# Pooled attention with an affine MLP block: the order of the first batch, and one of four products per batch moved to GpSimd

## The chip, the cores and the metric

The kernel runs on one core of a Trainium2 chip. A core has TensorE (PE in the profile; its weight loads are PEld), VectorE (DVE), ScalarE (ACT), GpSimd (POOL) and SyncE (SP), each with its own queue of instructions in program order; they wait for each other through semaphores. The metric is device time in microseconds (us), the median of several runs.

## The reference

Eight batches of eight heads, 576 positions, 64 values per head. k and v are averaged over groups of 8 positions, which leaves 72 keys. The attention of all 576 queries over these keys is the input x of an MLP block that first mixes tokens and then channels.

```
k_p, v_p = mean over 8 positions of k, v          # 72 of each
attn = softmax(q @ k_p^T / 8);   x = attn @ v_p    # 576 x 512 per batch
u = x + lam * (w_tok @ (alpha1 * x + beta1))
out = u + lam * (relu((alpha2 * u + beta2) @ w_ch1) @ w_ch2)
```

## The kernel before

The order of all instructions is written out by hand. Tokens are cut into chunks of 128: a batch has four chunks of its own and half of a fifth, which it shares with its neighbour. Four chunks are a block of the channel MLP, and there are nine blocks. The first batch (batch 0) has its attention ahead of all blocks, in straight-line code (lines 654 to 739). Block n then carries the attention of batch n+1 in its gaps. There the functions below are put on a list `todo` with a due time, in units of one step of TensorE work (0 to 15 are the 16 units of the first layer, `mlp_A`; 16 to 31 the quarters of the second, `mlp_B`), and the list is sorted by it and emitted (lines 792 to 824). The due times for a batch are in `attention(b)` (lines 742 to 790).

The steps of the attention, by name:

- `att_F` and `att_Frem` bring q into transposed form (in the first two batches with TensorE transposes, later with DMA). `cast_rem` makes bf16 of the last 64 rows of q and k.
- `sum_k` (GpSimd) adds up k, `att_K` (TensorE, then a copy) does the pooling of four heads. `double_k` prepares k in batch 0. `first_V` and `att_V` pool v.
- `att_S` or `att_S4` computes scores; ACT takes the exponential into ET.
- `att_AV(b, h)` multiplies with v for one head: five matmuls into ps_av, then DVE takes a reciprocal (L525) and writes x_tm (L527).
- `att_X(b, h0, h1)` multiplies two heads of x_tm with lam * alpha1 (`lamal_bc`), giving xs: a wide product of four chunks (L534) and a small one of the 64 rows of the fifth chunk (L538). Four calls make a batch, one per pair of heads.
- `mix_T(b, c)` is the token mix of one chunk: matmuls of wtT and xs (L567), DVE adds x (L571), and a product with alpha2 (L574) gives u_bf; `mix_uT` transposes it for `mlp_A`. `mix_T(b, 0)` needs all of xs.
- `setup_wtok(c)` transposes w_tok for chunk c (TensorE, then an ACT copy, L299); `setup_rowsum(c)` adds its row sums (L308, ACT copy L310), `setup_wtok_odd` makes the copy for odd batches (L316, L319, L320). `setup_bias(g)` computes beta2 through the first layer.
- `broadcast` spreads a vector over 128 partitions: a matmul with a row of ones into ps_bc, then ACT or DVE takes it out. `keep_warm(n)` issues n matmuls whose result nobody reads.

Buffers: x_tm has one buffer, PSUM has a ring of six that most steps share in the order of their allocation (`gp`), and two for the second layer (`ps_ch`). Loads on GpSimd's queue convert to bf16 on the way. Some loads are held back by a small memset on DVE (`behind`), so that they start at a chosen place of DVE's order.

Of the kernel before, what the change touches and what calls it, by code (L numbers as in the profile page):

```python
# [7 lines left out]
FP = mybir.dt.float32  # L8
# [3 lines left out]
ALU = mybir.AluOpType  # L12
# [11 lines left out]
def kernel(  # L24
# [116 lines left out]
    def cast_rem(b, eng, copy=None):  # L141
        raw = st1[b]["rem_raw"]
        rq = work.tile([P, 2, 2, D], BF, tag="rem_q", bufs=2, name="rem_q")
        rk = work.tile([P, 2, 2 if b else 3, D], BF, tag="rem_k", bufs=2, name="rem_k")
        (copy or eng.tensor_copy)(out=rq.rearrange("p c h d -> p h c d"), in_=raw[:, 0])  # L145
        twice = [raw[:, 1, :, c].unsqueeze(2).to_broadcast((P, 2, 2, D)) for c in range(2)]
        if b:
            eng.tensor_tensor(out=rk, in0=twice[0], in1=twice[1], op=ALU.add)
        st1[b]["rem"] = rq, rk
# [27 lines left out]
    al2_bc = const.tile([P, DM], FP, tag="al2_bc", name="al2_bc")  # L177
    b2row = const.tile([4, P], FP, tag="b2row", name="b2row")

    vecs = const.tile([65, 4, DM], FP, tag="vecs", name="vecs")  # L180
    ones_row = const.tile([1, P], FP, tag="ones_row", name="ones_row")
    nc.vector.memset(ones_row, 1.0)

    def load_vector(i, src, queue=nc.scalar):
        n = 65 if i in (0, 3) else 1
        queue.dma_start(out=vecs[0:n:64, i],
                        in_=src.unsqueeze(0).to_broadcast((1 + n // 65, DM)))

    new_batch(0)
    load_vector(0, moe_lam)  # L190
    load_rem(0)
    load_q_bf(0, 0)
    load_k16(0, 0)
    load_vector(1, moe_alpha1, nc.sync)
    load_vector(3, moe_beta1, nc.sync)
    start = const.tile([1, 2], FP, tag="start", name="start")
    nc.vector.memset(start, 0.0)
    nc.scalar.activation(out=start[:, 1:2], in_=start[:, 0:1], func=AF.Exp, bias=0.0, scale=1.0)
# [56 lines left out]

    def bias_row(i):
        p0 = 64 - 64 * i
        nc.vector.tensor_tensor(out=xs_pool[i][p0:p0 + 1, 4, :], in0=vecs[p0:p0 + 1, 3],
                                in1=vecs[p0:p0 + 1, 0], op=ALU.mult)

    b2c_bf = const.tile([P, 4], BF, tag="b2c_bf", name="b2c_bf")
# [3 lines left out]
    def more_constants():  # L265
        nc.vector.memset(ones_bf, 1.0)
        nc.vector.memset(ones_lo[0:64], 1.0)
        nc.vector.memset(ones_lo[64:128], 0.0)
        nc.vector.memset(wtT[:, :, S:640], 0.0)
# [2 lines left out]
        behind.memset(al2_bc[:, 0:1], 0.0)  # L272
        nc.sync.dma_start(out=al2_bc, in_=moe_alpha2.unsqueeze(0).to_broadcast((P, DM)))

    def broadcast(i, out, by=None):

        ps = gp("ps_bc")
        nc.tensor.matmul(out=ps, lhsT=ones_row, rhs=vecs[0:1, i])
        if by is None:
            nc.scalar.copy(out=out, in_=ps)  # L280
        else:
            nc.vector.tensor_tensor(out=out, in0=by, in1=ps, op=ALU.mult)

    def setup_vectors():
        ps = gp("ps_vec")
# [68 lines left out]
    def att_F(b, hp, copy=nc.scalar.copy):  # L354


        st = st1[b]
        u, r = hp // 2, hp % 2
        if r == 0:
            st["qT"][u] = work.tile([P, 8, P], BF, tag="qT", bufs=4, name="qT")  # L360
        if b > 1:
            if r == 0:
                nc.sync.dma_start_transpose(out=st["qT"][u],
                                            in_=st["q"][u].rearrange("p h c d -> p (h c d)"))
            return
        ps_q = gp("ps_q").bitcast(BF)
        for c in range(4):
            nc.tensor.transpose(
                out=ps_q[:, 128 * c:128 * c + 128],
                in_=st["q"][u][:, 2 * r + c // 2, 2 * (c % 2):2 * (c % 2) + 2].rearrange(  # L370
                    "p c d -> p (c d)"),
                identity=identity_bf)
        copy(out=st["qT"][u][:, 4 * r:4 * r + 4, :],
                       in_=ps_q[:, 0:512].rearrange("p (c t) -> p c t", c=4))
# [152 lines left out]
        nc.vector.tensor_tensor(out=x[:, 1 - odd:6 - odd, dd:dd + D], in0=av[:, :, 0:64],  # L527
                                in1=rec.unsqueeze(2).to_broadcast((P, 5, D)), op=ALU.mult)

    def att_X(b, h0, h1, eng=nc.vector):  # L530

        x, xs = st1[b]["x"], xs_pool[b % 2]
        cols = slice(D * h0, D * h1)
        eng.tensor_tensor(  # L534
            out=xs[:, 0:4, cols], in0=x[:, 1:5, cols],
            in1=lamal_bc[:, cols].unsqueeze(1).to_broadcast((P, 4, D * (h1 - h0))), op=ALU.mult)
        p0 = 64 * (b % 2)
        eng.tensor_tensor(out=xs[p0:p0 + 64, 4, cols], in0=x[p0:p0 + 64, 5 - 5 * (b % 2), cols],  # L538
                          in1=lamal_bc[p0:p0 + 64, cols], op=ALU.mult)


    st2 = {}
# [11 lines left out]
    def keep_warm(count):  # L554

        ps = psB.tile([P, DM], FP, tag="ch", bufs=2, name="ps_warm")
        for _ in range(count):
            nc.tensor.matmul(out=ps, lhsT=warm[:, 0:P], rhs=warm)
# [98 lines left out]
    load_q_bf(1, 0)  # L657
    load_q_bf(1, 1)
    load_w1(2)
    keep_warm(2)  # L660
    broadcast(0, lam_bc)
    keep_warm(2)
    att_F(0, 0)
    att_F(0, 1)
    more_constants()
    cast_rem(0, nc.vector)
    att_Frem(0, nc.scalar.copy)
    keep_warm(1)
    double_k(0)
# [10 lines left out]
    keep_warm(1)  # L680
    att_K(0, 1, None)
    att_AV(0, 1)
    broadcast(1, lamal_bc, lam_bc)
    att_F(0, 2)
    att_F(0, 3, nc.vector.tensor_copy)
    att_X(0, 0, 2, nc.gpsimd)
    att_AV(0, 2)
    keep_warm(1)
    att_S(0, 4)
    first_V(0, 1)  # L690
    att_AV(0, 3)
    att_X(0, 2, 4, nc.gpsimd)
    load_al2(nc.vector)
    att_S(0, 5)
    setup_vectors()
    keep_warm(1)
    att_AV(0, 4)
    att_S(0, 6)
    keep_warm(1)
    att_AV(0, 5)  # L700
    load_rem(1, behind=nc.vector)
    att_X(0, 4, 6, nc.gpsimd)
    att_S(0, 7)
    setup_wtok(0, nc.scalar.copy)
    att_AV(0, 6)
    setup_wtok(1, nc.scalar.copy)
    att_AV(0, 7)
    for u in range(2):
        load_k(1, u, nc.vector)
    setup_rowsum(0)  # L710
    setup_wtok(2, nc.scalar.copy)
    setup_rowsum(1)
    setup_wtok(3, nc.scalar.copy)
    att_X(0, 6, 8)
    setup_rowsum(2)
    keep_warm(1)
    load_w1(3)
    load_v16(1, (0, 1))
    setup_rowsum(3)
    mix_T(0, 0, nc.gpsimd)  # L720
    mix_T(0, 1, nc.gpsimd)
    load_v16(1, (2,))
    for g in range(3):
        load_w2(g)
    setup_bias(0)
    mix_T(0, 2)
    mix_uT((0, 0))
    mix_T(0, 3)
    setup_wtok(4, nc.scalar.copy)
    mix_uT((0, 1))  # L730
    setup_bias(1)
    mlp_A(0, 0, 0, 256)
    mix_uT((0, 2))
    mlp_A(0, 1, 0, 256)
    mlp_A(0, 2, 0, 256)
    mix_uT((0, 3))
    mlp_A(0, 3, 0, 256)
# [4 lines left out]
    def attention(b):  # L742


        first = b == 1
        todo = []
        if first:
            for hp in range(4):
                todo.append((2.6 + 0.9 * hp, lambda hp=hp: att_F(b, hp)))
            todo.append((3.5, lambda: cast_rem(b, nc.gpsimd)))  # L750
            todo.append((3.65, lambda: load_w2(3)))
            todo.append((7.4, lambda: att_Frem(b, nc.scalar.copy)))
        if b < B - 1:
            at = 27.0 if first else 10.0
            todo.append((at, lambda: att_F(b + 1, 0)))
            todo.append((at + 0.1, lambda: att_F(b + 1, 2)))
            at = 28.0 if first else 25.5
            todo.append((at - 1.0, lambda: cast_rem(b + 1, nc.gpsimd)))
            todo.append((at, lambda: att_Frem(b + 1)))
        for u in range(2):  # L760
            todo.append((3.6 + 0.1 * u if first else -0.9 + 1.2 * u,
                         lambda u=u: sum_k(b, u, nc.gpsimd)))
            todo.append((6.4 + 3.0 * u if first else 4.1 + 2.0 * u,
                         lambda u=u: att_K(b, u, nc.vector.tensor_copy)))
            if first:
                todo.append((11.0 + 1.2 * u, lambda u=u: first_V(b, u)))
        for u in range(2):
            at = (9.0 if first else 6.3, 13.6)[u]
            todo.append((at, lambda u=u: att_S4(b, u)))
            for k, dt in enumerate((0.1, 0.1, 0.1, 0.7, 1.7, 1.75) if u else (0.1, 0.1, 0.1, 1.1, 2.1, 3.1)):  # L770
                todo.append((at + dt, lambda u=u, k=k: st1[b]["exp", u](k)))
            for i, dt in enumerate((2.9, 3.4, 4.6, 5.1) if u else (5.7, 6.2, 2.9, 3.4)):
                h = 4 * u + i
                todo.append((at + dt, lambda h=h: att_AV(b, h)))
                if i % 2:
                    todo.append((at + dt + 0.1, lambda h=h: att_X(b, h - 1, h + 1)))
        if not first:
            for hp in range(4):
                todo.append((0.2 + 2.0 * hp, lambda hp=hp: att_V(b, hp)))
        for c in range(5):  # L780
            at = 21.0 + 1.3 * c
            if c < 4 or b % 2:
                todo.append((at, lambda c=c: mix_T(b, c)))
                key = (b, c) if c < 4 else (b - 1, 4)
                if first and c in (2, 3):
                    at += 1.3 * c - 2.0
                elif first and c < 2:
                    at += 1.0
                todo.append((at + 1.8, lambda key=key: mix_uT(key)))
        return todo  # L790
# [64 lines left out]
```

The softmax here doesn't subtract the row's maximum and nothing guards it: scores larger than these inputs give would overflow.

## Time and profile before

The median is 354.74 us (352.35 to 355.02, three runs). In the profiled execution the span is 351.1 us.

| engine | busy us | instructions |
|---|---|---|
| PE | 337.8 | 2206 |
| DVE | 226.0 | 476 |
| ACT | 150.6 | 283 |
| POOL | 78.9 | 93 |

| product xs (att_X) | count | us of one |
|---|---|---|
| DVE, wide, 128x512 | 29 | 0.69 |
| DVE, small, 64x128 | 29 | 0.29 |
| POOL, wide | 3 | 1.27 |
| POOL, small | 3 | 0.44 to 0.90 |

The span begins with the attention of batch 0; the first token mix starts at 23.99 us and the first layer of block 0 at 30.5 us. In the stretch from 0 to 50 us the DMA engines are nearly always busy. The table by engine is an average over all this: it says little about a wait in one place, for which the chain (what released each step) and the timeline of one engine have to be read.

### The profile page before, as it was taken

The numbers are of one execution on the slowest core, as the hardware profiler recorded it, in microseconds if no ns is written. First come the engines' busy times: TensorE is split into PE (matmuls) and PEld (weight loads), VectorE is DVE, ScalarE is ACT, GpSimd is POOL, SyncE is SP. The second block draws the span as 40 slices with busy tenths as digits, with TensorE's granted clock in tenths as the row PEclk, the third lists the DMA queues.
The fourth block names the chain that finished last, engine by engine and source line by source line (L and its number), as shares of the span: only waits on it lengthen the run. The fifth ranks groups of instructions, "written<-read, shape, count | busy, mean of one in ns | idle before, by whom it ended". The sixth has DMA issues, their size and how long they took to land.

```text
span 351.1 us, 5881 instructions
## 1 busy us (share of the span) xinstructions
PE 337.8 (96%) x2206; PEld 178.8 (51%) x2247; DVE 226.0 (64%) x476; ACT 150.6 (43%) x283; POOL 78.9 (22%) x93
## 2 busy tenths in 40 slices
PE   7989999999999999999999999999999999999995
PEld 2667654455544554455445544554455445545544
DVE  6564048788696769775967697948785883037511
ACT  4564972238502850087008800791069105703800
POOL 8578600072017000710071005300510000000000
PEclk9999999999999999999999999999999999999999
DMA  8999980898738942897189719991820032011012
GB/s 129 196 213 241 217 151 0 188 248 174 134 113 203 216 63 66 231 190 121 55 224 189 127 52 211 186 146 51 228 75 1 32 90 77 0 60 62 0 54 66
DMA packets 66045, 44.57 MB, mean 127 GB/s; under 512 B 32409, under 2 KB 57309, under 8 KB 66018
## 3 DMA queue, kind: packets, MB, share of 16 engines
q1 hardware_dynamic: 50486, 33.18, 39.4%
q0 software_dynamic: 15072, 10.76, 21.1%
q8 instruction: 17, 0.28, 0.3%
q10 hardware_dynamic: 460, 0.27, 0.3%
q14 instruction: 10, 0.08, 0.1%
HBM read 38.30 MB, written 9.44 MB: 136 GB/s over the span
## 4 chain that ended last, share of the span: by engine, by line
PE 85%; DVE 8%; ACT 3%; issue 2%; POOL 1%; POOLq 0%; DVEq 0%; ACTq 0%
PE ps_h L604 33%; PE ps_ch L638 30%; PE ps_tok L567 12%; DVE x_tm L527 2%; PE ps_s L475 2%; PE ps_av L519 2%; DVE xs L534 2%; DVE v_u L443 1%; PE ps_ch L627 1%; ACT wtT L299 1%; PE ps_kp L405 1%; DVE rec L525 1%; PE ps_sc L455 1%; DVE ps_ch L644 1%; PE ps_v L431 1%
## 5 line engine op out<-in xcount | busy, mean ns | idle before, releaser
L609 ACT ACTIVATE Hj<-ps_h,bias_cols 128x512 bf16<-128x512 f32 x144 | 98.4, 689 | 150.7 <-PE ps_h L604 149.2
L604 PE MATMUL ps_h<-u_fm,w 128*128 128x512 bf16 (+1 forms) x571 | 132.2, 374 | 2.0 <-ACT Hj L609 0.5
L638 PE MATMUL ps_ch<-w,Hj 128*128 128x512 bf16 x543 | 128.7, 379 | 1.1 <-issue 0.6
L604 PEld LDWEIGHTS <-w 128*128 128x128 bf16 x592 | 63.9, 114 | 52.4 <-issue 4.0
L638 PEld LDWEIGHTS <-Hj 128*128 128x128 bf16 x560 | 52.8, 98 | 60.9 <-issue 1.6
L567 PE MATMUL ps_tok<-xs,wtT 128*128 128x512 bf16 (+3 forms) x200 | 44.8, 380 | 1.9 <-DVE xs L534 1.8
L644 DVE TENSOR_TENSOR ps_ch<-lam_bc,ps_ch 128x512 f32<-128x512 f32 x32 | 22.2, 693 | 33.2 <-PE ps_ch L638 33.0
L145 POOL CAST rem_q<-rem_raw 128x256 bf16<-128x256 f32 x7 | 3.3, 475 | 151.6 <-DMA rem_raw<-in_q_dram 151.6
L571 DVE TENSOR_TENSOR u_sb<-x_tm,ps_tok 128x512 f32<-128x512 f32 (+1 forms) x40 | 27.3, 683 | 11.3 <-PE ps_tok L567 11.2
L527 DVE TENSOR_TENSOR x_tm<-ps_av,rec 128x320 f32<-128x320 f32 x64 | 31.5, 492 | 2.3
L645 DVE TENSOR_TENSOR u_sb<-u_sb,ps_ch 128x512 f32<-128x512 f32 x35 | 24.0, 687 | 13.7 <-PE ps_ch L638 12.5
L504 ACT ACTIVATE ET<-ps_s 72x512 f16<-72x512 f32 x56 | 32.3, 591 | 0.0
L525 DVE RECIPROCAL rec<-ps_av 128x5 f32<-128x5 f32 x64 | 12.2, 190 | 30.2 <-PE ps_av L523 30.0
L567 PEld LDWEIGHTS <-wtT 128*128 128x128 bf16 (+3 forms) x200 | 16.9, 100 | 23.6 <-DVE xs L534 3.4
L443 DVE TENSOR_TENSOR v_u<-v_u 72x512 f32<-72x512 f32 (+1 forms) x48 | 27.3, 570 | 0.8
L574 DVE TENSOR_TENSOR u_bf<-u_sb,al_bc 128x512 bf16<-128x512 f32 x34 | 25.8, 758 | 2.5 <-DMA u_fm<-u_bf 1.4
L160 POOL TENSOR_TENSOR k_raw<-k_raw 128x512 f32<-128x512 f32 x14 | 19.1, 1367 | 13.1 <-DMA k_raw<-in_k_dram 12.6
L534 DVE TENSOR_TENSOR xs<-x_tm,lamal_bc 128x512 bf16<-128x512 f32 x29 | 20.1, 692 | 1.0
L519 PEld LDWEIGHTS <-ET 72*128 72x128 f16 x256 | 14.1, 97 | 8.9 <-issue 0.4
L162 POOL TENSOR_TENSOR k_bf<-k_raw 128x512 bf16<-128x512 f32 x14 | 17.8, 1275 | 1.1
L519 PE MATMUL ps_av<-vp,ET 72*128 72x66 f16 x256 | 15.8, 193 | 0.2 <-issue 0.2
L417 DVE CAST kp<-ps_kp 128x288 bf16<-128x288 f32 x14 | 6.4, 456 | 12.9 <-PE ps_kp L411 12.3
(119 smaller groups left out, 228.0 us busy)
## 6 DMA issues: line engine op xcount, KB each, us to landing
out_dram<-u_sb SPq DMA_DIRECT2D x32, 256.0 KB
k_raw<-in_k_dram SPq DMA_DIRECT2D x14, 512.0 KB
v_u<-in_v_dram SPq DMA_DIRECT2D x12, 512.0 KB
q_bf<-in_q_dram POOLq DMA_DIRECT2D x16, 256.0 KB, 6.6
w<-in_moe_w_ch_dram POOLq DMA_DIRECT2D x8, 512.0 KB, 14.6
v<-in_v_dram POOLq DMA_DIRECT2D x4, 256.0 KB, 9.8
rem_raw<-in_q_dram SPq DMA_DIRECT2D x15, 64.0 KB
rem_raw<-in_k_dram SPq DMA_DIRECT2D x15, 64.0 KB
```

Source lines behind the costliest of these rows:

```text
L443: nc.vector.tensor_tensor(out=t[:, :, 0:n], in0=t[:, :, 0:n], in1=t[:, :, n:2 * n], op=ALU.add)
L504: nc.scalar.activation(out=o, in_=i, func=AF.Exp, bias=0.0, scale=0.125)
L519: nc.tensor.matmul(out=av[:, odd + c, :], lhsT=ET[:, m0:m0 + 128], rhs=vp1[:, hh, :])
L527: nc.vector.tensor_tensor(out=x[:, 1 - odd:6 - odd, dd:dd + D], in0=av[:, :, 0:64], in1=rec.unsqueeze(2).to_broadcast((P, 5, D)), op=ALU.mult)
L534: eng.tensor_tensor(out=xs[:, 0:4, cols], in0=x[:, 1:5, cols], in1=lamal_bc[:, cols].unsqueeze(1).to_broadcast((P, 4, D * (h1 - h0))), op= ...
L567: nc.tensor.matmul(out=ps_tok[p0:p1], lhsT=wtT[0:kk, at, P * c:P * c + p1 - p0], rhs=xs_pool[i][0:kk, sc, :], start=(sc == 0), stop=(sc == 4))
L571: nc.vector.tensor_tensor(out=s["u"][p0:p1, :], in0=x[p0:p1, 1 + c if c < 4 else 5 - 5 * i, :], in1=ps_tok[p0:p1, 0:DM], op=ALU.add)
L574: eng.tensor_tensor(out=s["u_bf"], in0=s["u"], in1=al2_bc, op=ALU.mult)
L604: nc.tensor.matmul(out=ps_h[:, t0:t1], lhsT=w1_of(cc, j), rhs=u_fm[n][:, cc, t0:t1], start=(cc == 0), stop=(cc == 3))
L609: nc.scalar.activation(out=t, in_=ps_h, func=AF.Relu, bias=bias_cols[:, j:j + 1], scale=1.0)
L638: nc.tensor.matmul(out=ps, lhsT=Hj[n, j][:, 128 * m:128 * m + 128], rhs=w2[j // 4][:, j % 4, :], start=(j == 0), stop=(j == NJ - 1))
L644: nc.vector.tensor_tensor(out=ps, in0=lam_bc, in1=ps, op=ALU.mult)
```

## The change

Three things are changed.

1. In the first batch the steps follow the order in which their inputs land. The rest of q and k is cast ahead of some memsets; `broadcast` is split into `spread_lam` and `spread_al1(half)`, which handles 256 columns at a time and is put where TensorE would wait; heads 4 to 7 are scored sooner; the transposes of w_tok, their row sums and the first mixes are interleaved anew. The small product of `att_X` becomes a function of its own, `rest_X`, and batch 0 does it once for all heads, on DVE. GpSimd makes u_bf for chunks 0 and 2 and no longer for 0 and 1. alpha1 is loaded through ACT's queue, beta1 takes its place on SP's.
2. In batches 1 to 7 the third pair of heads (`h == 5`) is multiplied by GpSimd and not by DVE.
3. In block 0 the second `att_K` is due at 8.2 and not at 9.4.

The aim is to take work off DVE's row ahead of the token mix, and to let the engines wait less in the first batch.

```
-    load_vector(1, moe_alpha1, nc.sync)
-    load_vector(3, moe_beta1, nc.sync)
+    load_vector(1, moe_beta1, nc.sync)
+    nc.scalar.dma_start(out=vecs[0:1, 2], in_=moe_alpha1.unsqueeze(0))
...
-    def broadcast(i, out, by=None):
+    def spread_lam():
...
+        nc.tensor.matmul(out=ps, lhsT=ones_row, rhs=vecs[0:1, 0])
+        nc.scalar.copy(out=lam_bc, in_=ps)
+    def spread_al1(half):
+        ps = gp("ps_bc")[:, 0:256]
+        cols = slice(256 * half, 256 * half + 256)
+        nc.tensor.matmul(out=ps, lhsT=ones_row, rhs=vecs[0:1, 2, cols])
+        nc.vector.tensor_tensor(out=lamal_bc[:, cols], in0=lam_bc[:, cols], in1=ps, op=ALU.mult)
...
-    def att_X(b, h0, h1, eng=nc.vector):
+    def rest_X(b, h0, h1, eng=nc.vector):
...
+    def att_X(b, h0, h1, eng=nc.vector, rest=True):
...
+        if rest:
+            rest_X(b, h0, h1, eng)
...
-    keep_warm(2)
-    broadcast(0, lam_bc)
-    keep_warm(2)
+    keep_warm(3)
+    spread_lam()
+    keep_warm(3)
     att_F(0, 0)
     att_F(0, 1)
+    cast_rem(0, nc.vector)
     more_constants()
-    cast_rem(0, nc.vector)
+    keep_warm(1)
     att_Frem(0, nc.scalar.copy)
...
     att_AV(0, 1)
-    broadcast(1, lamal_bc, lam_bc)
     att_F(0, 2)
     att_F(0, 3, nc.vector.tensor_copy)
-    att_X(0, 0, 2, nc.gpsimd)
+    spread_al1(0)
+    att_X(0, 0, 2, nc.gpsimd, False)
+    att_S(0, 4)
     att_AV(0, 2)
-    keep_warm(1)
-    att_S(0, 4)
+    spread_al1(1)
+    att_S(0, 5)
     first_V(0, 1)
     att_AV(0, 3)
-    att_X(0, 2, 4, nc.gpsimd)
+    att_X(0, 2, 4, nc.gpsimd, False)
     load_al2(nc.vector)
-    att_S(0, 5)
+    att_S(0, 6)
     setup_vectors()
+    att_AV(0, 4)
     keep_warm(1)
-    att_AV(0, 4)
-    att_S(0, 6)
-    keep_warm(1)
+    att_S(0, 7)
     att_AV(0, 5)
     load_rem(1, behind=nc.vector)
-    att_X(0, 4, 6, nc.gpsimd)
-    att_S(0, 7)
+    att_X(0, 4, 6, nc.gpsimd, False)
     setup_wtok(0, nc.scalar.copy)
+    setup_wtok(1, nc.scalar.copy)
     att_AV(0, 6)
-    setup_wtok(1, nc.scalar.copy)
+    setup_rowsum(0)
     att_AV(0, 7)
     for u in range(2):
         load_k(1, u, nc.vector)
-    setup_rowsum(0)
     setup_wtok(2, nc.scalar.copy)
     setup_rowsum(1)
+    setup_bias(0)
     setup_wtok(3, nc.scalar.copy)
-    att_X(0, 6, 8)
-    setup_rowsum(2)
-    keep_warm(1)
+    att_X(0, 6, 8, nc.vector, False)
+    rest_X(0, 0, H)
     load_w1(3)
     load_v16(1, (0, 1))
+    mix_T(0, 0, nc.gpsimd)
+    setup_rowsum(2)
+    mix_T(0, 1)
     setup_rowsum(3)
-    mix_T(0, 0, nc.gpsimd)
-    mix_T(0, 1, nc.gpsimd)
     load_v16(1, (2,))
-    for g in range(3):
+    load_w2(0)
+    mix_T(0, 2, nc.gpsimd)
+    for g in range(1, 3):
         load_w2(g)
-    setup_bias(0)
-    mix_T(0, 2)
     mix_uT((0, 0))
     mix_T(0, 3)
+    mix_uT((0, 1))
     setup_wtok(4, nc.scalar.copy)
-    mix_uT((0, 1))
     setup_bias(1)
     mlp_A(0, 0, 0, 256)
+    mlp_A(0, 1, 0, 256)
     mix_uT((0, 2))
-    mlp_A(0, 1, 0, 256)
     mlp_A(0, 2, 0, 256)
...
-            todo.append((6.4 + 3.0 * u if first else 4.1 + 2.0 * u,
+            todo.append((6.4 + 1.8 * u if first else 4.1 + 2.0 * u,
                          lambda u=u: att_K(b, u, nc.vector.tensor_copy)))
...
-                    todo.append((at + dt + 0.1, lambda h=h: att_X(b, h - 1, h + 1)))
+                    eng = nc.gpsimd if h == 5 else nc.vector
+                    todo.append((at + dt + 0.1, lambda h=h, eng=eng: att_X(b, h - 1, h + 1, eng)))
```

More of the change, by code (lines that the diff above doesn't have):

```diff
@@ L178 @@
     b2row = const.tile([4, P], FP, tag="b2row", name="b2row")
-    vecs = const.tile([65, 4, DM], FP, tag="vecs", name="vecs")
+    vecs = const.tile([65, 3, DM], FP, tag="vecs", name="vecs")
     ones_row = const.tile([1, P], FP, tag="ones_row", name="ones_row")
@@ L184, in load_vector @@
     def load_vector(i, src, queue=nc.scalar):
-        n = 65 if i in (0, 3) else 1
-        queue.dma_start(out=vecs[0:n:64, i],
-                        in_=src.unsqueeze(0).to_broadcast((1 + n // 65, DM)))
+        queue.dma_start(out=vecs[0:65:64, i], in_=src.unsqueeze(0).to_broadcast((2, DM)))
     new_batch(0)
@@ L257, in bias_row @@
         p0 = 64 - 64 * i
-        nc.vector.tensor_tensor(out=xs_pool[i][p0:p0 + 1, 4, :], in0=vecs[p0:p0 + 1, 3],
+        nc.vector.tensor_tensor(out=xs_pool[i][p0:p0 + 1, 4, :], in0=vecs[p0:p0 + 1, 1],
                                 in1=vecs[p0:p0 + 1, 0], op=ALU.mult)
@@ L273, in load_al2 @@
         nc.sync.dma_start(out=al2_bc, in_=moe_alpha2.unsqueeze(0).to_broadcast((P, DM)))
-    def broadcast(i, out, by=None):
+    def spread_lam():
         ps = gp("ps_bc")
[L278 to L282, printed above, removed]
+        nc.tensor.matmul(out=ps, lhsT=ones_row, rhs=vecs[0:1, 0])
[5 more added lines that the diff above has]
+        nc.vector.tensor_tensor(out=lamal_bc[:, cols], in0=lam_bc[:, cols], in1=ps, op=ALU.mult)
     def setup_vectors():
@@ L528, in att_AV @@
                                 in1=rec.unsqueeze(2).to_broadcast((P, 5, D)), op=ALU.mult)
-    def att_X(b, h0, h1, eng=nc.vector):
+    def rest_X(b, h0, h1, eng=nc.vector):
+        x, xs = st1[b]["x"], xs_pool[b % 2]
+        cols, p0 = slice(D * h0, D * h1), 64 * (b % 2)
+        eng.tensor_tensor(out=xs[p0:p0 + 64, 4, cols], in0=x[p0:p0 + 64, 5 - 5 * (b % 2), cols],
+                          in1=lamal_bc[p0:p0 + 64, cols], op=ALU.mult)
+    def att_X(b, h0, h1, eng=nc.vector, rest=True):
         x, xs = st1[b]["x"], xs_pool[b % 2]
@@ L536, in att_X @@
             in1=lamal_bc[:, cols].unsqueeze(1).to_broadcast((P, 4, D * (h1 - h0))), op=ALU.mult)
-        p0 = 64 * (b % 2)
-        eng.tensor_tensor(out=xs[p0:p0 + 64, 4, cols], in0=x[p0:p0 + 64, 5 - 5 * (b % 2), cols],
-                          in1=lamal_bc[p0:p0 + 64, cols], op=ALU.mult)
+        if rest:
+            rest_X(b, h0, h1, eng)
     st2 = {}
```

## The prediction

> **What bounds the kernel now.** I read the engine line of the page first.
>
> ```profile
> PE 337.8 (96%) x2206; PEld 178.8 (51%) x2247; DVE 226.0 (64%) x476; ACT 150.6 (43%) x283; POOL 78.9 (22%) x93
> ```
>
> PE is busy for 337.8 of 351.1 us, so only about 13 us can be won by removing PE waits, and some 5 us of these are the first 1.4 us and the last output transfer. Everything else the change can win must be a PE gap, or a stretch at the start in which PE is busy with fillers while another engine sets the pace. The table of waits of PE names the gaps (in us: total, times, longest).
>
> ```profile
> PE ps_tok L567 <- DVE xs L534: 1.8, 4, 0.6
> PE ps_rs L308 <- ACT wtT L299: 1.1, 3, 0.6
> PE ps_h L604 <- ACT Hj L609: 0.5, 1, 0.5
> ```
>
> The first is the token mix waiting for the products xs; the timeline puts its four gaps at 59.55 (0.63 us), 133.00 (0.40), 205.19 and 277.38 (0.4 each), all in odd batches. The chain around the first (start, us, what) shows why: DVE has a solid row of work from 53.16 on, and the third pair's products (the two lines at 56.39 and 57.10) stand in it.
>
> ```profile
> 56.39 0.69 DVE xs L534
> 57.10 0.29 DVE xs L538
> ...
> 58.80 0.70 DVE xs L534
> 59.51 0.04 issue
> 59.55 1.24 PE ps_tok L567 x5
> ```
>
> The chain of the start, same columns: from 19.1 to 23.7 us the last thing waited for is ACT, first the exponentials of heads 6 and 7, then the copies of the transposed w_tok. The first token mix begins only behind the fourth row sum.
>
> ```profile
> 19.12 1.37 ACT ET L460 x4
> 20.50 1.18 ACT wtT L299 x2
> ...
> 22.97 0.70 ACT wtT L299
> 23.67 0.04 issue
> 23.71 0.44 PE ps_rs L308 x5
> 24.15 0.86 PE ps_tok L567 x4
> ```
>
> From there to 35.0 us PE is dense (10.4 of 10.85 us busy). In block 0, the chain around the third gap: unit 10 of the first layer waits for the ReLU of unit 9, which stood behind two copies for the odd w_tok.
>
> ```profile
> 41.95 0.54 ACT wtT L319
> ...
> 42.51 0.67 ACT wtT L320
> ...
> 43.20 0.70 ACT Hj L609
> 43.90 0.04 issue
> 43.94 0.38 PE ps_h L604
> ```
>
> Last the timeline of POOL (start, us, operation): the second half of batch 1's k lands at 37.94 and is summed by 40.55.
>
> ```profile
> 21.89 0.90 POOL L538 TENSOR_TENSOR xs<-x_tm,lamal_bc 64x128 bf16<-64x128 f32 x1
> 37.94 1.26 POOL L160 TENSOR_TENSOR k_raw<-k_raw 128x512 f32<-128x512 f32 x1 [1.18 <-DMA k_raw<-in_k_dram]
> 39.28 1.27 POOL L162 TENSOR_TENSOR k_bf<-k_raw 128x512 bf16<-128x512 f32 x1
> ```
>
> **What the Trainium skill says.** "SBUF — State Buffer", section on the two separate sides: GpSimd and VectorE share a port pair under an exclusive lock, which a VectorE operation with two SBUF inputs contends for. The trace agrees: POOL's small product at 21.89 took 0.90 us against 0.44 and 0.45 for its two sisters, and the DVE one beside it at 22.41 took 0.54 against 0.29; three POOL products beside DVE operations that read PSUM kept 1.27 us. "TensorE: Matmul & The Clock Gate", Part 1: PE runs at half rate until a busy window of about 3.4 us that is free-running. Here 256-column matmuls took 0.21 us each until about 12.2 us, 0.11 us after. "DMA: Bandwidth & Descriptors", section on queues, rings and completion order: each DMA engine goes round robin over the queues. From 30 to 33 us the two queues moved 0.35 and 0.38 MB, so k keeps its share whatever GpSimd has queued.
>
> **The change, part by part.**
>
> 1. *Third pair to GpSimd, seven batches.* DVE loses 0.69 + 0.29 = 0.98 us of the row that ends at 59.49 (and at 132.94 and so on). GpSimd needs 1.27 + 0.45 = 1.72 us (rows of the first batch). It was idle there: no POOL instruction stands between 42 and 72 us, nor in 122 to 136. In block 0 the products start at 56.45, after head 5's x_tm ends at 56.37, and end at 58.2. DVE does two reciprocals and two x_tm in this time, which read PSUM, then wants to start its last product at 58.80 - 0.98 = 57.82. If the lock holds it until 58.2, it ends at 58.9; unheld at 58.5. PE comes free at 58.92. So the 0.63 goes, and the three of 0.4 (in which 0.6 of slack is won at least). Even batches had no wait: nothing. **-1.8 us.** The new wait: behind GpSimd's products stand, in block 0, the two loads of q for batch 2, which were issued at 40.5 and now go at about 58. DMA moved nothing from 52 to 62, and their transposes are issued at 74.3: hidden. In later blocks only cast_rem stands behind, which waits for a DMA anyway.
>
> 2. *The first batch.* alpha1's product in two halves: PE 2 x 0.53 us for 1.05; DVE 2 x 0.35 to 0.42 (nearest row: 128x256 from PSUM, 0.42; pitch of a 128x512: 0.60) for 0.60. GpSimd's three small products (1.8 us) go, DVE's one of 64x128 becomes one of 64x512 (0.69 by the 128x512 row). cast_rem ahead of the memsets lets ps_qr start about 0.2 us sooner, filled with warm-up matmuls. From the kpT copy, which I put at 14.6 (14.80 before), DVE needs the old 7.68 us (14.80 to 22.48) less 0.25 idle, plus 0.15: its last wide product ends at 22.2. PE must have issued three w_tok transposes, two row sums and bias 0 by then. With heads 4 to 7 scored earlier, ACT reaches the first copy at 19.3 to 20.0 instead of 20.5, and row sum 0 follows at 21.5; the third and fourth row sums are no longer ahead of the mix. bias 0 needs w1's first part, landed at 20.6 (issued 9.29, 11.3 us). The first mix starts at 22.4 (22.2 to 22.8) instead of 23.99: **-1.6 us**. Its last matmul needs the 64x512 product at 22.9, and comes 0.87 us in, so that is hidden. The work from there to 35.0 is the same (bias 0 goes ahead, row sums 2 and 3 come in, 0.5 each). Two ACT waits in it, 0.17 at 30.51 and 0.24 at 33.10, mostly go: **-0.4 us**.
>
> 3. *k pooled sooner.* att_K(1,1) goes from behind att_S4(1,0) to ahead of the odd transposes. The buffer that unit 10 takes is then that of the transposes (free at 42.48 by the old clock) and not unit 9's: the gap of 0.46 goes, **-0.5 us**. But PE would reach it at 41.00 - 2.0 = 39.0 us, and the summed k is there at 40.55, or 0.4 to 0.5 sooner since the gates of the transfers on DVE move up a little with head 3 and 5. The transfers cannot follow by 2 us, the queue was full from 20 to 36 us. A new PE wait of 1.0 us (0.5 to 1.6): **+1.0 us**. Behind it stand the odd transposes, unit 9 and the scores of batch 1.
>
> 4. The merged vector tile, alpha1 on ACT's queue (0.45 us of issue ahead of the table load; lam_bc's copy slips by 0.3, needed only at 15) and al2's load: no path, they lie under PE's warm-up.
>
> Sum: -1.8 - 1.6 - 0.4 - 0.5 + 1.0 = -3.3 us; 354.74 - 3.3 = **351.4**. PE is dense after each gap, so gains carry to the end one for one.
>
> **Rivals.**
> *A, more.* The fillers leave no PE gap from 1.4 to 8.8 us, the clock comes up one window (3.4 us) sooner; the half-rate work on the path from 8.8 to 12.2 (about 2.4 us) halves. -1.2, and the k transfers start sooner too, so the new wait goes: -3.3 - 1.2 - 1.0 = -5.5, **349.2**. For: idle 2.26 to 2.88 and 6.9 to 7.7 is filled. Against: the phase of the window is chance, and transposes may not count.
> *B, start gains nothing.* The ring of six PSUM buffers makes PE wait for DVE before head 7's scores, ACT ends as late as before, and the mix starts at 24. Left: -0.5 - 1.8 = -2.3, **352.4**. For: DVE was nearly solid from 14.8 to 22.95, and gets 0.15 + 0.40 more. Against: ACT's waits of 1.15, 0.36 and 0.63 between 14.8 and 18.2 are what the new order fills.
> *C, slower.* GpSimd becomes the last. If its products take the longest seen, 1.74 (the k sum at 76.31, beside two-input DVE work) + 0.90 = 2.64 us, they end at 59.1 in block 0 and hold DVE's last product to 59.8 instead of 59.49: +0.3 in seven batches, +2.1. The two q loads (0.5 MB at 200 GB/s, 2.6 us) then meet the burst of v and k from 62 on, and batch 2's second k sum (ready 79.46, used 80.92) comes 1.1 us late: +3.2 in all, **357.9**. Against: GpSimd is otherwise idle, and DVE has only PSUM-reading work for 1.4 us.
>
> **How the numbers follow.** The forecast 0.50, A 0.20, B 0.18, C 0.12. 1% is 3.55 us, hence 351.2 and 358.3: the forecast lies at that line, so I split it evenly; A is faster, B the same, C goes to slower for most. Faster 0.45, same 0.45, slower 0.10. Range 348.9 to 355.2: it takes in A and B and the spread of the three times before (352.35 to 355.02), and leaves out C and the far side of A.
>
> **What the changed profile would show.** Step 1: "ps_tok <- DVE xs" gone from PE's waits, xs of 128x512 on POOL 10 times at about 1.27 us, no PE gap ahead of any first mix. Step 2: the first ps_tok near 22.4 us, the second layer-one half (16 matmuls of 256 columns) ending near 33.0. Step 3: no ps_h wait for Hj near 42, and a wait of ps_kp for POOL's k_bf of about 1 us near 39. It would be wrong if the clock comes up at another time, if the k transfer lands at another time (a step of 1 us either way), or if the lock makes GpSimd's products longer than 2 us.

## The result, and the profile after

The changed kernel takes 349.94 us (349.43 to 350.17, four runs) beside 354.31 us of the kernel before; the ratio is 0.988, with an interval of 0.984 to 0.993. Measured again later beside the experiments: 349.86 and 353.37 us, ratio 0.990 (0.988 to 0.992). So 3.5 to 4.4 us less, for a forecast of 3.3. The profiled span fell from 351.1 to 347.7 us. Executions at a lower granted clock, or far above the others of the same kernel, are left out of all medians here and below.

The page's engine line: PE has 1.4 us less to do by its count, and 3.4 us less span to do it in; GpSimd has 11 us more.

```profile
PE 336.4 (97%) x2208; PEld 178.9 (51%) x2249; DVE 219.8 (63%) x463; ACT 150.3 (43%) x283; POOL 89.7 (26%) x104
```

PE's waits of the changed kernel (total, times, longest). The token mix waits for xs once, for 0.2 us, and not four times for 1.8; the wait for a ReLU is gone. Behind the first mix, a small wait for k_bf is new, which was forecast, and that of the scores for kp has grown from 0.17 to 1.2 us, which was not. (Ahead of it PE now waits 0.4 us once for q, and 0.3 and 0.2 for kpT.)

```profile
PE ps_s L477 <- DVE kp L419: 1.2, 1, 1.2
...
PE ps_kp L407 <- POOL k_bf L162: 0.3, 1, 0.3
...
PE ps_tok L575 <- DVE xs L543: 0.2, 1, 0.2
```

PE's timeline at five places of it (start, us, operation, idle before): the first token mix, the second pooling of k, the units 10 and 11 of block 0, the first mix of batch 1, the scores of batch 2.

```profile
22.25 1.25 PE L575 MATMUL ps_tok<-xs,wtT 128*128 128x512 bf16 x4 [0.17 <-DVE xs L543]
...
39.48 0.29 PE L407 MATMUL ps_kp<-pool_main,k_bf 128*128 128x64 bf16 x4 [0.28 <-POOL k_bf L162]
...
41.81 1.92 PE L612 MATMUL ps_h<-u_fm,w 128*128 128x512 bf16 x8
...
56.65 1.24 PE L575 MATMUL ps_tok<-xs,wtT 128*128 128x512 bf16 x5
...
79.53 0.30 PE L477 MATMUL ps_s<-qT,kp 64*72 64x256 bf16 x2 [1.19 <-DVE kp L419]
```

The same place in the kernel before, for the last line:

```profile
81.41 0.30 PE L475 MATMUL ps_s<-qT,kp 64*72 64x256 bf16 x2 [0.17 <-DVE kp L417]
```

Set against the same places of before, these starts make a ledger:

| place | before | after | lead |
|---|---|---|---|
| first token mix | 23.99 | 22.25 | 1.74 |
| unit 10, block 0 | 43.94 | 41.81 | 2.13 |
| first mix, batch 1 | 59.55 | 56.65 | 2.90 |
| scores, batch 2 | 81.41 | 79.53 | 1.88 |
| first mix, batch 3 | 133.00 | 130.63 | 2.37 |
| first mix, batch 5 | 205.19 | 202.33 | 2.86 |
| first mix, batch 7 | 277.38 | 274.03 | 3.35 |
| end | 351.1 | 347.7 | 3.4 |

The lead grows at each place where a gain was forecast, and falls by 1.02 us between batch 1's mix and batch 2's scores. GpSimd's timeline, first a line of before and then the changed kernel, shows what is new ahead of that fall: its products, and behind them the two q loads of batch 2, which stood at 40.49 before.

```profile
40.49 1.54 POOL L77 DMA_DIRECT2D q_bf<-in_q_dram x2
```

```profile
54.33 1.27 POOL L543 TENSOR_TENSOR xs<-x_tm,lamal_bc 128x512 bf16<-128x512 f32 x1 [14.91 <-DVE x_tm L529]
55.68 0.86 POOL L536 TENSOR_TENSOR xs<-x_tm,lamal_bc 64x128 bf16<-64x128 f32 x1
56.50 1.57 POOL L77 DMA_DIRECT2D q_bf<-in_q_dram x2
...
71.88 1.27 POOL L160 TENSOR_TENSOR k_raw<-k_raw 128x512 f32<-128x512 f32 x1 [0.54 <-DMA k_raw<-in_k_dram]
```

The chain ahead of the wait (start, us, what): DVE's sums of v take 1.72, 1.39 and 1.25 us. Later ones of the same sizes take 0.69, 0.46 and 0.29; the slow ones run beside GpSimd's sums of k. The kp copy stands behind them.

```profile
73.34 1.72 DVE v_u L445
...
75.08 1.39 DVE v_u L445
...
76.49 1.25 DVE vp L447
...
79.03 0.46 DVE kp L419
79.49 0.04 issue
79.53 0.30 PE ps_s L477 x2
```

This contention isn't new. In the kernel before DVE's last sum beside GpSimd was as slow, and PE waited 0.17 us:

```profile
78.36 1.25 DVE L445 TENSOR_TENSOR vp<-v_u 72x128 f16<-72x128 f32 x1
```

What is new is the date: PE has a lead of 2.9 us, but GpSimd ends its sums of k only 1.9 us sooner (77.58 against 79.46), and DVE's sum ends with them.

### The profile page after: what moved, and what is told of

Same layout as the page of the kernel before. It is cut to its first block, busy times and chain, and to the rows that moved or that the text cites. A ratio compares the mean times of both kernels' runs of the same rounds, so it can differ in the third digit from the quotient of the medians.

```text
span 347.7 us, 5897 instructions
## 1 busy us (share of the span) xinstructions
PE 336.4 (97%) x2208; PEld 178.9 (51%) x2249; DVE 219.8 (63%) x463; ACT 150.3 (43%) x283; POOL 89.7 (26%) x104
## 4 chain that ended last, share of the span: by engine, by line
PE 89%; DVE 4%; POOL 2%; DMA 2%; issue 2%; ACT 1%; POOLq 0%; DVEq 0%
PE ps_ch L646 34%; PE ps_h L612 33%; PE ps_tok L575 12%; PE ps_av L521 2%; PE ps_s L477 2%; DMA q_bf<-in_q_dram 2%; DVE v_u L445 1%; PE ps_ch L635 1%; DVE ps_ch L652 1%; PE ps_r L484 1%; PE ps_uT L596 1%; PE ps_av L525 1%; PE ps_kp L407 0%; PE ps_q L370 0%; DVE u_sb L653 0%
## 5 line engine op out<-in xcount | busy, mean ns | idle before, releaser
L575 PE MATMUL ps_tok<-xs,wtT 128*128 128x512 bf16 (+2 forms) x199 | 44.8, 380 | 0.5 <-DVE xs L543 0.2
L652 DVE TENSOR_TENSOR ps_ch<-lam_bc,ps_ch 128x512 f32<-128x512 f32 x32 | 22.2, 693 | 35.0 <-PE ps_ch L646 34.7
L543 POOL TENSOR_TENSOR xs<-x_tm,lamal_bc 128x512 bf16<-128x512 f32 x10 | 12.7, 1268 | 118.5 <-DVE x_tm L529 115.9
L445 DVE TENSOR_TENSOR v_u<-v_u 72x512 f32<-72x512 f32 (+1 forms) x48 | 28.4, 591 | 0.8
L582 DVE TENSOR_TENSOR u_bf<-u_sb,al_bc 128x512 bf16<-128x512 f32 x34 | 24.2, 711 | 1.3 <-DMA u_fm<-u_bf 0.2
L543 DVE TENSOR_TENSOR xs<-x_tm,lamal_bc 128x512 bf16<-128x512 f32 x22 | 15.4, 701 | 0.7
```

The lines of the kernel that those rows point to most:

```text
L445: nc.vector.tensor_tensor(out=t[:, :, 0:n], in0=t[:, :, 0:n], in1=t[:, :, n:2 * n], op=ALU.add)
L543: eng.tensor_tensor(out=xs[:, 0:4, cols], in0=x[:, 1:5, cols], in1=lamal_bc[:, cols].unsqueeze(1).to_broadcast((P, 4, D * (h1 - h0))), op= ...
L575: nc.tensor.matmul(out=ps_tok[p0:p1], lhsT=wtT[0:kk, at, P * c:P * c + p1 - p0], rhs=xs_pool[i][0:kk, sc, :], start=(sc == 0), stop=(sc == 4))
L582: eng.tensor_tensor(out=s["u_bf"], in0=s["u"], in1=al2_bc, op=ALU.mult)
L652: nc.vector.tensor_tensor(out=ps, in0=lam_bc, in1=ps, op=ALU.mult)
```

## The experiments

Each kernel was timed beside the kernel before, and the ratios are to it. Where two others are compared with each other by time, they were timed together.

**1. The q loads early (q_early).** Theory: the displaced loads meet the burst of v, rest and k. Rival: it is the shared port alone. The edit to the changed kernel:

```
-                    at = (21.0 if b == 1 else 0.4) + 0.1 * u
+                    at = (10.0 if b == 1 else 0.4) + 0.1 * u
                     todo.append((at, lambda b=b, u=u: load_q_bf(b + 1, u)))
```

> The changed kernel with the two q loads of batch 2 ahead of GpSimd's products in block 0 (due 10.0, as they ran before at 40 us). Theory (displaced loads): they met the burst of v, rest and k loads from 58 us on and made k 1.2 us later against PE. Then they are issued near 39.5, k's sums start 1 us sooner, the wait of ps_s for kp (1.19 at 79.53) falls to 0.2, and the span goes from 347.7 to 346.7. Rival (lock only): DVE's sums of v merely fall behind GpSimd's sums of k on the shared port, whatever the loads do: the wait stays within 0.3 of 1.19 and the span at 347.7.

349.12 us, ratio 0.9885 (0.9855 to 0.9914). The wait for kp was gone, but in this trace the first mix started only at 24.76 us, so the span (348.5) tells nothing. It was run again beside the changed kernel itself.

> The changed kernel again, so that the others of this call are compared with it on one chip. The wait of ps_s for kp near 80 us is again 1.2 us; the ratio to the kernel before is 0.988 to 0.991.

> The changed kernel with the two q loads of batch 2 early, timed beside the changed kernel. Displaced loads: 1.0 to 1.2 us less than the changed kernel (ratio to it 0.997), with no wait of ps_s for kp. If the wait only moves elsewhere, the same time within 0.3 us. The first token mix may start anywhere from 22.0 to 24.8 us, by when the clock comes up, so the traces are to be compared from that start on.

The changed kernel: 349.86 us, wait for kp 1.16. With the loads early: 348.93 us, ratio 0.9871 (0.9849 to 0.9893), span 346.9 against 348.2, no wait for kp. That is 0.9 us, forecast 1.0 to 1.2; the two intervals overlap, but the six times of the second (348.61 to 349.46) lie below all six of the first (349.61 to 350.30). GpSimd's timeline with the loads early: they go at 39.61, and k's sum starts 1.1 us sooner than at 71.88, without a wait for its transfer.

```profile
39.61 1.54 POOL L77 DMA_DIRECT2D q_bf<-in_q_dram x2
...
70.77 1.27 POOL L160 TENSOR_TENSOR k_raw<-k_raw 128x512 f32<-128x512 f32 x1
```

The DMA queues from 60 to 62 us say why. In the changed kernel the software queue, which carries q, holds the engines:

```profile
q0 software_dynamic: 583, 0.28, 110.5%
q1 hardware_dynamic: 85, 0.17, 22.9%
```

With the loads early the hardware queue, which carries v and k, is alone:

```profile
q1 hardware_dynamic: 139, 0.25, 51.5%
```

In the changed kernel the v loads were issued at 58.83 and moved nothing before 61.2 us, when q was nearly through. With the q loads early they were issued at 59.09 and moved data from 59.2 on. The k loads, next on SP's queue, were issued at 65.85 and at 64.47.

The rival holds a part: the loss is paid where DVE's v sums lie beside GpSimd's k sums. But with k 1.1 us sooner GpSimd is done with k at 76.29, and the v sum at 76.61 takes 0.29 us and not 1.25:

```profile
76.61 0.29 DVE L447 TENSOR_TENSOR vp<-v_u 72x128 f16<-72x128 f32 x1
```

**2. The third pair back on DVE (x_on_dve).** Edit: `eng = nc.vector` in place of `nc.gpsimd if h == 5 else nc.vector`.

> The changed kernel with the third pair back on DVE in batches 1 to 7. Both theories: the four waits of the token mix for xs come back (0.63 and three of 0.4, 1.8 us). Displaced loads: the q loads go early again, so the 1.19 at 79.53 goes, and the span is 347.7 + 1.8 - 1.0 = 348.5. Lock only: the 1.19 stays and the span is 349.5.

351.65 us, ratio 0.9955 (0.9939 to 0.9971); span 349.2. The four waits are back and the one for kp is gone, which the rival did not allow:

```profile
PE ps_tok L575 <- DVE xs L543: 1.8, 4, 0.6
```

**3. Only the third pair on GpSimd, on the kernel before (x_alone).** Edit: the last two lines of the diff, and nothing else.

> The kernel before with only the third pair of batches 1 to 7 on GpSimd. By the prediction's step 1: the four waits of ps_tok for xs (1.8 us) go, span 351.1 - 1.8 = 349.3. Displaced loads take a part back: the wait of ps_s for kp grows from 0.17 to 0.5 to 1.2, so span 349.6 to 350.3, ratio to before 0.996 to 0.998.

351.36 us, ratio 0.9940 (0.9917 to 0.9963): 2.0 us, more than the forecast of 0.8 to 1.5. The trace's span is 1.6 us less. All waits for xs are gone, and the displaced loads show here too, as the wait at 81.28 us (0.17 before). The two make 1.0 us; the rest isn't in these waits (see 7).

```profile
PE ps_s L475 <- DVE kp L417: 1.0, 1, 1.0
```

The start is that of the kernel before (first mix at 23.78 us), so the new start isn't what made the loads collide. They were issued at 58.40, and v, issued at 60.74, again moved nothing before 63.2 us. In the kernel before v began to move data at about 62 us: it would have met them there too.

**4. Only the order of the first batch (start_alone).** Edit: the changed kernel with the third pair on DVE and `6.4 + 3.0 * u`.

> The change with only the new order of the first batch (third pair on DVE, k at its old place). By step 2: first token mix at 22.0 to 22.8, the four waits for xs (1.8) and the one for Hj (0.5) as before, none for kp at 80: 1.9 us less than before, ratio 0.9946. If the start's gain is taken back by the landing of k or v, the ratio is 0.998.

351.87 us, ratio 0.9960 (0.9947 to 0.9973): 1.5 us, where 1.9 were expected; by the trace 1.9 (span 349.2). First mix at 22.02; the old waits for xs and for Hj are there, none for kp.

**5. Only k pooled sooner (k_alone), and k late in the changed kernel (k_late).** Edits: 3.0 to 1.8 in the kernel before, and back to 3.0 in the changed one.

> The kernel before with only the second pooling of k in block 0 at 8.2. By step 3: with the old start PE gets there at 41.0 us and the summed k at 40.55, so no wait or 0.1; the wait for Hj ahead of unit 10 (0.46, with its tail 0.6) goes: span 350.6, ratio 0.9985. If the transfer lands later than in the first trace, a wait of up to 0.6 takes the gain back.

352.71 us, ratio 0.9978 (0.9964 to 0.9993): 0.8 us. The wait for Hj is gone, none for k_bf came. The span of this trace (351.4) shows no gain, since PE waited 0.63 us at 110.69 for the transposed u of batch 2.

> The changed kernel with the second pooling of k in block 0 at 9.4 again. By the prediction's step 3 the wait for Hj ahead of unit 10 (0.46) comes back and the wait for k_bf (0.28) goes: unit 10 starts at 41.8 + 0.2 to 0.3, span 347.9. Rival (ACT had caught up in the new order): no wait for Hj, unit 10 0.3 sooner, span 347.4. A later wait in block 1 may hide either.

350.42 us, ratio 0.9916 (0.9888 to 0.9944). The wait for Hj is back, as step 3 had it, and that for k_bf is gone:

```profile
43.76 1.89 PE L612 MATMUL ps_h<-u_fm,w 128*128 128x512 bf16 x8 [0.46 <-ACT Hj L617]
```

How its time compares with that of the changed kernel stays unclear: the two weren't timed together, and the intervals overlap.

**6. Fewer fillers at the start (few_fillers).** Rival A of the prediction said an earlier clock would be worth 1.2 us more. In the changed trace it did come up early: the filler at 7.81 us took 0.38 us, against 0.59 at 9.31 in the kernel before. Edit: `keep_warm(2)` twice for `keep_warm(3)`, and the one ahead of `att_Frem` out.

> The changed kernel with 2 and 2 fillers around the spread of lam instead of 3 and 3, and none ahead of ps_qr. If the fillers bring the clock up one window sooner (7.7 us and not 12.2), it comes up at 11 to 12.5 here: 256-column scores near 10 us then take 0.21 apiece. If that early clock is worth what rival A of the prediction said, the first token mix starts 1.0 to 1.2 us later (23.3). If DVE and the landings of the loads set the start, it stays at 22.3 to 22.6 and the span at 347.7 to 348.1.

350.02 us, ratio 0.9898 (0.9869 to 0.9927). A filler still takes 0.59 us at 9.23, so the clock came up over 1.5 us later than in the changed trace, and yet the first mix starts at 22.04, sooner than 22.25. Two lines of the few-filler trace, the first mix and the pooling of k:

```profile
22.04 1.26 PE L575 MATMUL ps_tok<-xs,wtT 128*128 128x512 bf16 x4 [0.17 <-DVE xs L543]
...
40.06 0.29 PE L407 MATMUL ps_kp<-pool_main,k_bf 128*128 128x64 bf16 x4 [1.09 <-POOL k_bf L162]
```

The early clock bought nothing here: in the changed trace PE runs into the landing of the second q load at 13.79 (0.36 us of wait), and in the trace of few fillers it comes at 13.59 and doesn't wait. The second trace of the changed kernel agrees: a filler at 8.09 still took 0.63 us, and the first mix started at 22.22. A very late clock seems to cost: in the first q_early trace matmuls were at half rate until about 15 us, and the first mix came at 24.76. That is one trace, in which the first q landed 0.66 us later too.

**7. Even batches on DVE again (q_early_odd).** Edit on q_early: `h == 5 and b % 2`.

> As q early, with the third pair on GpSimd in odd batches only. By the prediction's step 1 the even batches had no wait for xs and gain nothing: the same time within 0.2 us. Rival: in even batches GpSimd's relief of DVE helps elsewhere (or its wait costs), then 0.3 us or more apart.

> The changed kernel with the q loads early, a third time, as the partner of the others in this call: ratio to the kernel before 0.987 to 0.9885.

350.27 us, ratio 0.9894 (0.9869 to 0.9918), beside 348.82 us, ratio 0.9856 (0.9828 to 0.9884), of q early in all batches. So the even batches are worth about 1.4 us where I expected nothing, though the intervals overlap. 1.1 us of it lies within the spans, whose medians are 348.2 and 347.1. The trace, set beside that of q_early_again, shows 0.6 us as one wait for the transposed u of batch 2:

```profile
108.85 1.03 PE L612 MATMUL ps_h<-u_fm,w 128*128 128x512 bf16 x4 [0.63 <-DMA u_fm<-u_bf]
```

About 0.1 us more goes in each of the three even batches: the first mixes of batches 4 and 6 come 36.62 us behind those ahead of them, and 36.50 with GpSimd. This trace's first mix started 0.7 us later. That the wait of 0.6 belongs to the edit isn't shown. The same wait stands in the trace of k_alone, where DVE has the third pair in all batches, a shorter one (0.23, in batch 4) in the second trace of the changed kernel, where GpSimd has it, and none in those of before and x_on_dve. What makes the transpose land late is open: in q early it was issued 12.25 us after that batch's first mix, here 12.06, and there was no wait.

**8. The best version (q_early_k88).** The wait for k_bf was 0.28, 0.40 and 0.70 us for first mixes at 22.25, 22.22 and 22.08, and 1.09 at 22.04. A faster start brings PE here sooner, but k's own date counts as much: in the last of these traces it was summed from 37.40 us, in the others from 36.81 to 37.06. So the pooling was put behind the odd transposes, where unit 10 still doesn't need unit 9's buffer: q early with `6.4 + 2.4 * u`.

> The changed kernel with the q loads of batch 2 early and the second pooling of k in block 0 at 8.8, behind the odd transposes of w_tok and still ahead of unit 9. The wait for k_bf shrinks by the 0.45 us of the transposes and the wait for Hj stays away, since unit 10 then takes the buffer of this pooling: 0.3 to 0.5 us less than q early alone where the start was quick. If the wait for Hj comes back all the same, no gain.

348.28 us, ratio 0.9844 (0.9815 to 0.9872), the fastest of all; span 346.5. It is 0.5 us below q early (348.82), as expected, though the intervals overlap. PE passes this place without a wait, for k_bf or for Hj, in a trace whose first mix started at 22.44:

```profile
39.28 0.52 PE L318 MATMUL ps_wo<-identity_bf,wt_bf 128*128 128x128 bf16 x5
39.83 0.29 PE L407 MATMUL ps_kp<-pool_main,k_bf 128*128 128x64 bf16 x4
...
40.01 1.03 PE L612 MATMUL ps_h<-u_fm,w 128*128 128x512 bf16 x4
```

## Why the prediction was right, and where not

The time (351.4 forecast, 349.94 measured, 3.3 us against 3.5 to 4.4) was right, and most of it by the forecast's own mechanism: xs off DVE's row, the start in the order of the landings. That the total came so close is partly luck, as errors of 0.5 to 1.0 us cancelled. By its steps:

**Step 1, the odd batches: right.** The four waits of 1.8 us are gone, and come back when the edit is undone. GpSimd's wide product took 1.27 us as priced. The lock was met, but it was not DVE's wide product that was held: that one ran from 55.54 to 56.23, and GpSimd's small product beside it took 0.86 us and not 0.45. GpSimd ended at 56.54, PE arrived at 56.65.

**Step 1, the q loads behind it: wrong.** "DMA moved nothing from 52 to 62 ... hidden" gave the loads no duration and read the gap by the old clock. Issued at 56.50, they took 4.1 to 4.9 us to land and moved data until about 62, and the v loads had moved forward with the lead, to 58.83. x_alone shows that the first of the two errors is enough. Nor did "k keeps its share whatever GpSimd has queued" carry over to v: from 58.83 to 61.2 it moved nothing. It cost 1.0 us. This is like the second half of rival C, which came without its first half: in no odd batch did PE wait for GpSimd. C priced the two loads at 2.6 us, and had k's second sum come too late for its own pooling; here that pooling ran at 78.03, and PE waited for DVE. C's sum is also wrong: its 357.9 leaves out the gains of steps 2 and 3.

**Step 1, the even batches: wrong in size.** "No wait: nothing" was worth about 1.4 us with q early. The traces place about 0.1 us in each even batch; where the rest comes from is open.

**Step 2: right.** The first mix at 22.25 (forecast 22.4, 22.2 to 22.8), and 22.0 to 22.8 in all traces with the new start but two (24.76 and 24.03, both with a later clock or a fall of it). Of the two ACT waits behind it one (0.17) went and the other (0.24) stayed; the first halves ended at 33.04 (forecast 33.0). Rival B is out.

**Step 3: the mechanism right, one term too large.** The gap of 0.46 went in the changed kernel and returned in k_late. The new wait for k_bf was 0.28 us and not 1.0: the second half of k was summed from 36.81, 1.1 us sooner than before (37.94), where I allowed 0.4 to 0.5. About half of that is scatter. In the two other traces with the old start it was summed from 37.42 and 37.49, and in the eight whose first mix started at 22.0 to 22.8 from 36.81 to 37.40: on average 0.5 us sooner, as allowed. The gates on DVE had moved by 0.3 (21.71 to 21.42).

**Rival A:** its premise came true in the first trace of the changed kernel, its gain did not: PE runs into the landing of q, and the first mix waits 0.17 us for DVE's xs there as it does in the trace of few fillers. The fillers alone don't bring the early clock, as the last section shows.

By the ledger, the errors cancelled: 1.0 us was lost to the q loads, and against it stand 0.7 for k_bf and about 0.5 more than forecast at the odd mixes and in the even batches.

## What to carry to other kernels

When work is moved to an idle engine, read its queue behind the new instruction: here two loads went from 40 to 57 us with it, which cost half of what the move won in odd batches, and giving them an earlier place got it back. Before calling a transfer hidden in a gap of the DMA, add its duration to its issue (here 4 to 5 us to land), and date the end of the gap by what gates the next burst, since a change that wins time moves that too. A load whose landing hardly moves turns a faster start into a wait, so place its user behind other ready work.

## What the runs showed of the hardware

The time at which TensorE reaches full rate varied from run to run of nearly the same code: about 7.8 us in the changed trace, about 9 in its second one, 11 in that of x_on_dve with the same start, 12 in the one of before, about 15 in the first q_early one. In the k_late trace it fell back: a pair of 256-column score matmuls took 0.39 us at 13.27 and 0.63 at 19.54, and ten w_tok transposes 1.26 us at 20.33 where the changed trace has 0.72.

Two DMA queues with work did not always share. From 30 to 33 us of the kernel before the software queue moved 0.35 MB and the hardware queue 0.38. But a load on the hardware queue moved nothing for 2.4 us (58.83 to 61.2 in the changed kernel; 60.74 to 63.2 in x_alone) while the software queue moved the 0.5 MB of q. What decides between the two isn't shown.

GpSimd and DVE slowed each other where both read two operands from SBUF: GpSimd's 64x128 product took 0.86 us beside a DVE product (55.68 us of the changed kernel) and 0.44 without one (17.93 us of before), DVE's 72x128 sum 1.25 us beside GpSimd's sum of k (76.49) and 0.29 without it (78.82).
